# Gated linear attention by a cumulative log-decay over each chunk, in front of a two-expert router

## The chip, the cores and the metric

The kernel runs on one core of a Trainium2 chip. Its time is the device time of one execution in microseconds (us); the metric is the median of the runs.

## The reference

The first half is a gated linear recurrence for 4 batches, 8 heads, 768 tokens and 48 channels a head. The second half sends every token to its two best of 8 experts.

```
f = sigmoid(f_logit)                        # f_logit: normal, mean 2, spread 0.5
for t in range(S):
    state = f[t][:, None] * state + outer(k[t], v[t])     # 48 x 48 for each batch and head
    y[t]  = q[t] @ state
x = y, heads side by side                   # 3072 tokens x 384
noisy = x @ w_gate + softplus(x @ w_noise) * noise
top2 of noisy, weights = softmax over the two
out = sum over the two experts of weight * relu(x @ w1[e]) @ w2[e]     # 384 -> 1024 -> 384
```

All numbers are 32-bit floats.

## The kernel before, in words

The tokens are cut into 6 chunks of 128 per batch, so there are 24 pieces (chunk `c`, batch `b`), each with all 8 heads. Two heads share the 128 partitions (rows 0 to 47 and 64 to 111), so a piece has four pairs of heads, laid side by side as 4 x 128 columns.

**One piece** (`chunk`, L151 to L256). The sync queue SP loads `f`, `q`, `k`, `v`, the first three into one of three sets of padded tiles. TensorE (PE) transposes `f`, `q` and `k` (L166), four transposes each; ScalarE (ACT) takes the sigmoid (L170). The scores inside the chunk are built in seven levels, l = 0 to 6. Level l computes for each head the product of half the queries (64 columns) with the keys (L205), and VectorE (DVE) copies those that belong to the level into the score matrix `A` through a mask (L211; the last level by ACT, L213). Between levels the queries are multiplied by products of the decays on DVE (L215), and the keys and the decay products on GpSimd (POOL, L217, L219). A separate product gives the diagonal (L189, L191). A 32-bit matmul stands in the trace as two instructions, a transpose as one, so a level has 16 of them. Then `y` is made from `A` and `v` (L226) and from the carried state (L230, not for c = 0), and the state is carried on: the keys are transposed back (L240), multiplied with `v` (L247), and the old state is scaled and added (L254, L255; not in the last chunk).

**The order.** `by_turns` lets two streams of pieces alternate, two batches in each; it yields after the diagonal, after every level and after `y`. When the four pieces of a chunk are done, `pack` moves `y` by 10 DMAs into rows of 128 features (L265), and `route` (L270) transposes it to tokens, writes it out (`x_rows`), computes the router's logits (L285), the top two (a softplus out of Exp and Ln, then an Exp, L290 to L303), and scatters the tokens into expert lists by 8 indirect DMAs of the POOL queue (L343). The next chunk follows. Instructions of one engine run in the order in which the tile framework's scheduler has put them, near the program's order.

**The experts.** `plan` (L350) turns the counts into 55 tiles of 128 list entries. For each tile the token rows are gathered (L395), transposed (L407), sent through both layers (L417, L431), and added to the output rows (L426, L434, L436). Weights are fetched three tiles ahead (L401, L402). The output is cleared at the start by 24 DMAs that the POOL queue issues (L454).

PSUM is eight banks of 2 KB a partition: four single ones under the name `one`, two pairs under `two`.

Of the kernel before, what the change touches and what calls it, by code (L numbers as in the profile page):

```python
# [8 lines left out]
F32 = mybir.dt.float32  # L9
U8 = mybir.dt.uint8  # L10
U32 = mybir.dt.uint32
# [6 lines left out]

@with_exitstack
def kernel(  # L20
    ctx: ExitStack,
    tc: tile.TileContext,
    q: bass.AP,
    k: bass.AP,
    v: bass.AP,
    f_logit: bass.AP,
    moe_w_gate: bass.AP,
    moe_w_noise: bass.AP,
    moe_noise: bass.AP,
    moe_w1: bass.AP,  # L30
    moe_w2: bass.AP,
    out: bass.AP,
):

# [23 lines left out]
    C = 128  # L58
# [7 lines left out]
    TB = B * C  # L66
    NB = (2 * N - E) // 128 + E
    NR = 3
    FAR = 1 << 20
    assert (H * D, H * DP, 1 << NL, B * S) == (DM, 512, C, N) and TB == 512  # L70
# [4 lines left out]
    rt = ctx.enter_context(tc.tile_pool(name="rt", bufs=2))  # L75
    ffn = ctx.enter_context(tc.tile_pool(name="ffn", bufs=3))
# [29 lines left out]

    def counting(name, pattern, base=0, by_partition=0):
        t = const.tile([128] + [n for _, n in pattern], F32, tag=name, name=name)
        nc.gpsimd.iota(t, pattern=pattern, base=base, channel_multiplier=by_partition,
                       allow_small_or_imprecise_dtypes=True)  # L110
        return t

    iota = counting("iota", [[1, E]])
    list_of = counting("list_of", [[N, E]])
    token = counting("token", [[C, NCH], [S, B]], by_partition=1)
    start_of = counting("start_of", [[128, N // 128]])
    block = counting("block", [[1, NB]])

    ones = const.tile([128, 128], F32, tag="ones", name="ones")
    nc.gpsimd.memset(ones, 1.0)  # L120
    earlier = const.tile([128, 128], F32, tag="earlier", name="earlier")
    nc.gpsimd.affine_select(out=earlier, in_=ones, compare_op=ALU.is_ge, fill=0.0, base=-1,
                            pattern=[[1, 128]], channel_multiplier=-1)


    LR = E * N + 128
    x_rows = tc.dram_tile([N, DM], F32, name="x_rows")
    lists = tc.dram_tile([LR, 4], U32, name="lists")
    empty = const.tile([128, LR // 128, 4], U32, tag="empty", name="empty")
    for i, val in enumerate((0, FAR, 0, FAR)):  # L130
        nc.vector.memset(empty[:, :, i], val)
    nc.sync.dma_start(out=lists.rearrange("(p r) w -> p r w", p=128), in_=empty)

# [9 lines left out]

    xT = [None] * NCH
    before = const.tile([128, NCH * B + 1, E], F32, tag="before", name="before")
    nc.vector.memset(before[:, 0, :], 0.0)
    state = [None] * B
# [122 lines left out]
    def route(c):  # L270
        def t(shape, tag, dtype=F32):
            return rt.tile([128] + shape, dtype, tag=tag, name=f"{tag}_{c}")

        for b in range(B):
            xp = one_bank(f"xp_{c}_{b}")
            for i in range(KO):
                nc.tensor.transpose(xp[:, i * 128:(i + 1) * 128], xT[c][:, i, b * C:(b + 1) * C], ident)
            xs = t([DM], "xs")
            nc.scalar.copy(xs, xp[:, 0:DM])
            nc.sync.dma_start(out=x_rows[b * S + c * C:b * S + (c + 1) * C, :], in_=xs)  # L280

        lg = one_bank(f"lg_{c}")[:, 0:B * 2 * E].rearrange("t (b e) -> t b e", b=B)
# [11 lines left out]
        nc.vector.tensor_tensor(sp, sp, noise[:, c], ALU.mult)  # L294
        nc.vector.tensor_tensor(nz, sp, lg[:, :, 0:E], ALU.add)
        mx, ix, fx = t([B, 8], "mx"), t([B, 8], "ix", U32), t([B, 8], "fx")
        for b in range(B):
# [141 lines left out]

    def by_turns(*streams):  # L440
        streams = [iter(x) for x in streams]
        while streams:
            for x in list(streams):
                if next(x, streams) is streams:
                    streams.remove(x)

    def chunks(c, bs):
        for b in bs:
            yield from chunk(c, b)

# [59 lines left out]
```

## Time and profile before

| | |
|---|---|
| runs | 1420.2, 1413.39, 1419.17 us; median 1419.17 |
| profiled execution | 1423.89 us, its span 1422.2 us |
| mean granted clock of TensorE | 0.783 of full speed |
| PE busy | 1178.9 us (83%), 8391 instructions |
| ACT / DVE / POOL busy | 189.6 / 357.8 / 448.1 us |
| attention, to the last matmul of `y` | 0 to 692.8 us |
| from there to the first matmul of the experts | 692.8 to 740.1 us |
| experts | 740.1 to 1422.2 us |

The busy share alone says that TensorE is nearly full, but it is a mean over two very different stages: in the attention most of TensorE's instructions use a part of the array at half the clock, in the experts they use all of it at nearly the full clock.

### The profile page before, as it was taken

The numbers are of one execution on the slowest core, as the hardware profiler recorded it, in microseconds if no ns is written. First come the engines' busy times: TensorE is split into PE (matmuls) and PEld (weight loads), VectorE is DVE, ScalarE is ACT, GpSimd is POOL, SyncE is SP. The second block draws the span as 40 slices with busy tenths as digits, with TensorE's granted clock in tenths as the row PEclk, the third lists the DMA queues.
The fourth block names the chain that finished last, engine by engine and source line by source line (L and its number), as shares of the span: only waits on it lengthen the run. The fifth ranks groups of instructions, "written<-read, shape, count | busy, mean of one in ns | idle before, by whom it ended". The sixth has DMA issues, their size and how long they took to land. (4 is left out here: it accounts for less than half of the span.)

```text
span 1422.2 us, 21155 instructions
## 1 busy us (share of the span) xinstructions
PE 1178.9 (83%) x8391; PEld 953.1 (67%) x8391; DVE 357.8 (25%) x814; ACT 189.6 (13%) x322; POOL 448.1 (32%) x663
## 2 busy tenths in 40 slices
PE   3596797799599689789728889998989989999997
PEld 3585685666477568577526667776777767777775
DVE  2362552543345255245120000010100000011000
ACT  1013012111210301211100101010111101011110
POOL 9741430531323233062031222322222222222331
PEclk9976555555555555565559999999999999999999
DMA  9124022221211402210144635427163453637110
GB/s 194 54 46 86 5 45 56 35 45 35 56 23 24 90 1 45 56 18 6 36 162 148 211 124 192 142 90 245 45 215 128 143 196 118 234 109 256 51 40 7
DMA packets 163107, 135.64 MB, mean 95 GB/s; under 512 B 115909, under 2 KB 144249, under 8 KB 163008
## 3 DMA queue, kind: packets, MB, share of 16 engines
q1 hardware_dynamic: 149184, 104.34, 25.7%
q0 software_dynamic: 13824, 29.94, 6.9%
q8 instruction: 67, 1.10, 0.3%
q14 instruction: 32, 0.26, 0.1%
HBM read 213.75 MB, written 20.74 MB: 165 GB/s over the span
## 5 line engine op out<-in xcount | busy, mean ns | idle before, releaser
L417 PEld LDWEIGHTS hp<-xt,w 128*128 128x128 f32 x2640 | 317.6, 197 | 49.9 <-ACT hs L420 34.5
L417 PE MATMUL hp<-xt,w 128*128 128x128 f32 x2640 | 327.5, 282 | 23.9 <-ACT hs L420 23.3
L205 PE MATMUL sc<-qP,kQ 48*128 48x64 f32 (+1 forms) x2688 | 274.0, 392 | 82.4 <-DVE A L191 43.3
L205 PEld LDWEIGHTS sc<-qP,kQ 48*128 48x128 f32 (+1 forms) x2688 | 263.2, 301 | 93.0 <-DVE A L191 44.7
L431 PE MATMUL yp<-w,hs 128*128 128x384 f32 x880 | 294.6, 488 | 0.0
L431 PEld LDWEIGHTS yp<-w,hs 128*128 128x128 f32 x880 | 163.7, 191 | 102.9 <-issue 1.7
L211 DVE COPY_PREDICATED A<-masks,sc 128x512 f32<-128x512 uint8 x144 | 130.5, 906 | 115.2 <-PE sc L205 86.1
L420 ACT ACTIVATE hs<-hp 128x512 f32<-128x512 f32 x110 | 65.7, 597 | 631.3 <-PE hp L417 623.7
L436 POOL DMA_INDIRECT out_dram<-ys,slots x55 | 55.6, 1011 | 295.8 <-DVE ys L434 295.4
L434 DVE SCALAR_TENSOR_TENSOR ys<-yp,slots,had 128x384 f32<-128x384 f32 x55 | 34.0, 618 | 446.1 <-PE yp L431 314.7
L217 POOL TENSOR_TENSOR kQ<-kQ,T 128x256 f32<-128x256 f32 x140 | 94.8, 677 | 137.4 <-PE sc L205 137.2
L343 POOL DMA_INDIRECT lists<-entry,sloti x48 | 46.9, 977 | 208.6 <-DVE sloti L340 195.8
L426 POOL DMA_INDIRECT had<-out_dram,slots x55 | 57.0, 1036 | 174.6 <-issue 138.3
L409 DVE COPY xt<-xgp 128x384 f32<-128x384 f32 x55 | 30.7, 558 | 183.5 <-PE xgp L407 183.5
L407 PE MATMUL xgp<-ident,xg 128*128 128x128 f32 x165 | 29.7, 291 | 49.5 <-DMA xg<-x_rows,slots 49.5
L215 DVE TENSOR_TENSOR qP<-qP,T 128x256 f32<-128x256 f32 x144 | 62.2, 432 | 11.3 <-PE sc L205 10.4
L395 POOL DMA_INDIRECT xg<-x_rows,slots x55 | 53.4, 971 | 30.7 <-issue 19.4
L226 PE MATMUL y<-A,v 128*48 128x128 f32 x384 | 60.1, 428 | 0.0
L213 ACT COPY A<-sc 64x512 f32<-64x512 f32 x24 | 13.9, 578 | 336.8 <-DVE qP L215 326.1
L407 PEld LDWEIGHTS xgp<-ident,xg 128*128 128x128 f32 x165 | 20.3, 148 | 51.7 <-issue 32.2
L230 PE MATMUL y<-qP,st 48*48 48x128 f32 x320 | 53.3, 432 | 0.0
L226 PEld LDWEIGHTS y<-A,v 128*48 128x48 f32 x384 | 25.1, 175 | 26.5 <-issue 25.0
(119 smaller groups left out, 767.6 us busy)
## 6 DMA issues: line engine op xcount, KB each, us to landing
w<-in_moe_w_dram SPq DMA_DIRECT2D x110, 1536.0 KB
f<-in_f_logit_dram SPq DMA_DIRECT2D x24, 192.0 KB
q<-in_q_dram SPq DMA_DIRECT2D x24, 192.0 KB
k<-in_k_dram SPq DMA_DIRECT2D x24, 192.0 KB
v<-in_v_dram SPq DMA_DIRECT2D x24, 192.0 KB
out_dram<-zero POOLq DMA_DIRECT2D x24, 192.0 KB, 2.2
x_rows<-xs SPq DMA_DIRECT2D x24, 192.0 KB
xT<-yT SPq DMA_DIRECT2D x36, 96.0 KB
```

Source lines behind the costliest of these rows:

```text
L205: nc.tensor.matmul(sc[0:nj, par, hp * HC:(hp + 1) * HC].rearrange("j (a m) -> j a m", m=m), lhsT=kQ[rows(par), hp * C:hp * C + nj], rhs=qv ...
L211: nc.vector.copy_predicated(Av, masks[:, l].rearrange("j (r x m) -> j r x m", r=2, m=m), scv)
L215: nc.vector.tensor_tensor(qv, qv, Tv[:, :, 0:1].broadcast_to((128, x, m)), ALU.mult)
L217: nc.gpsimd.tensor_tensor(kv, kv, Tv[:, :, 1:2].broadcast_to((128, x, m)), ALU.mult)
L226: nc.tensor.matmul(y[rows(par), par, cols(hp)], lhsT=vt[:, 2 * hp + par, :], rhs=A[:, par, cols(hp)], start=True, stop=(c == 0))
L230: nc.tensor.matmul(y[rows(par), par, cols(hp)], lhsT=state[b][rows(par), hp, :], rhs=qP[rows(par), cols(hp)], start=False, stop=True)
L395: nc.gpsimd.indirect_dma_start(out=xg, out_offset=None, in_=x_rows, in_offset=bass.IndirectOffsetOnAxis(ap=slots[:, 0:1], axis=0))
L417: nc.tensor.matmul(hp[:, fo // 4, fo % 4, :], lhsT=w1[t % NR][:, i, fo * 128:(fo + 1) * 128], rhs=xt[:, i, :], start=(i == 0), stop=(i == ...
L420: nc.scalar.activation(hs[:, fo - 3:fo + 1, :], hp[:, fo // 4], AF.Relu)
L426: nc.gpsimd.indirect_dma_start(out=had, out_offset=None, in_=out, in_offset=bass.IndirectOffsetOnAxis(ap=slots[:, 1:2], axis=0), bounds_ch ...
L431: nc.tensor.matmul(yp[:, 0:DM], lhsT=hs[:, fo, :], rhs=w2[t % NR][:, fo, :], start=(fo == 0), stop=(fo == FO - 1))
L436: nc.gpsimd.indirect_dma_start(out=out, out_offset=bass.IndirectOffsetOnAxis(ap=slots[:, 3:4], axis=0), in_=ys, in_offset=None, bounds_che ...
```

## The change

The seven levels are replaced by one product. With L the running sum of -ln(f) inside the chunk, the decay from key j to query i is exp(-(L_i - L_j)). So the queries are multiplied by P = exp(-L), the keys by Q = exp(L), one matmul per head gives all 128 x 128 scores, and one multiplication with a causal mask makes `A`. L comes from Exp, Ln (ACT) and a running sum along the columns (`tensor_tensor_scan` on DVE, which starts again at each pair of heads and is capped at 60). The state is carried as P at the chunk's end times (old state + keys times `v`).

The pieces run as five stages with a lag each, in one loop over 24 steps and a few more, and `pack` is gone: the logits are computed straight from `y` with the router's weights laid out by pairs of heads, for each piece as it comes, in one PSUM bank that is held from the first batch's piece to `route`. The loads are four sets deep. At the very end a register is loaded and a branch decides on a redo of everything by the general method: it is taken if any channel's sum over a chunk exceeded 39. `plan` and all of the experts' part keep their text.

```diff
+    def load(n):
+        c, b = n // B, n % B
+        for nm, src in (("f", f_logit), ("q", q), ("k", k), ("v", v)):
+            nc.sync.dma_start(out=pads[nm][n % NLD][:, :, 0:D],
+                              in_=src[b, :, c * C:(c + 1) * C, :].rearrange("h t d -> t h d"))
...
+    def forget(n):
+        raw = pads["f"][n % NLD].rearrange("t h d -> t (h d)")
+        nc.gpsimd.tensor_scalar(raw, raw, XMIN, None, ALU.max)
+        f = wk.tile([128, HP * C], F32, tag="f", name=f"f_{n}")
+        nc.scalar.activation(f, transposed("f", n), AF.Exp, scale=-1.0)
+        nc.scalar.activation(f, f, AF.Ln, bias=1.0)
+        L = wk.tile([128, HP * C], F32, tag="L", name=f"L_{n}")
+        top = cap[n % 2]
+        nc.gpsimd.tensor_copy(top[:, :, 0], f.rearrange("d (a t) -> d a t", t=C)[:, :, 0])
+        nc.vector.tensor_tensor_scan(L, data0=f, data1=top.rearrange("d a t -> d (a t)"), initial=0.0,
+                                     op0=ALU.add, op1=ALU.min)
+        P[n] = wk.tile([128, HP * C], F32, tag="P", name=f"P_{n}", bufs=4)
+        nc.scalar.activation(P[n], L, AF.Exp, scale=-1.0)
+        Q[n] = wk.tile([128, HP * C], F32, tag="Q", name=f"Q_{n}")
+        nc.scalar.activation(Q[n], L, AF.Exp)
+        nc.gpsimd.tensor_copy(far[:, n, :], L.rearrange("d (a t) -> d a t", t=C)[:, :, C - 1])
+    def scaled(n):
+        qP[n] = wk.tile([128, HP * C], F32, tag="qP", name=f"qP_{n}", bufs=3)
+        nc.vector.tensor_tensor(qP[n], transposed("q", n), P[n], ALU.mult)
+        kQ[n] = wk.tile([128, HP * C], F32, tag="kQ", name=f"kQ_{n}")
+        nc.vector.tensor_tensor(kQ[n], transposed("k", n), Q[n], ALU.mult)
+    def scores(n):
+        sc = two_banks(f"sc_{n}")
+        for hp in range(HP):
+            for par in range(2):
+                nc.tensor.matmul(sc[:, par, cols(hp)], lhsT=kQ[n][rows(par), cols(hp)],
+                                 rhs=qP[n][rows(par), cols(hp)], start=True, stop=True)
+        A[n] = wk.tile([C, 2, HP * C], F32, tag="A", name=f"A_{n}")
+        nc.vector.tensor_tensor(A[n].rearrange("j r (a i) -> j (r a) i", i=C), sc.rearrange("j r (a i) -> j (r a) i", i=C),
+                                causal.unsqueeze(1).broadcast_to((C, H, C)), ALU.mult)
+        if n // B < NCH - 1:
+            kp = one_bank(f"kp_{n}")
+            for hp in range(HP):
+                nc.tensor.transpose(kp[:, cols(hp)], kQ[n][:, cols(hp)], ident)
+            kn[n] = wk.tile([C, H, DP], F32, tag="kn", name=f"kn_{n}")
+            nc.scalar.copy(kn[n].rearrange("t h d -> t (h d)"), kp)
+    def output(n):
+        c, b = n // B, n % B
+        vt = pads["v"][n % NLD]
+        y = one_bank(f"y_{n}")
+        for hp in range(HP):
+            for par in range(2):
+                nc.tensor.matmul(y[rows(par), cols(hp)], lhsT=vt[:, 2 * hp + par, :], rhs=A[n][:, par, cols(hp)],
+                                 start=True, stop=(c == 0))
+            if c:
+                for par in range(2):
+                    nc.tensor.matmul(y[rows(par), cols(hp)], lhsT=state[b][rows(par), hp, :],
+                                     rhs=qP[n][rows(par), cols(hp)], start=False, stop=True)
+        yT[n] = wk.tile([128, HP * C], F32, tag="yT", name=f"yT_{n}")
+        nc.scalar.copy(yT[n], y)
+        if c == NCH - 1:
+            return
+        ds = one_bank(f"ds_{n}")
+        for hp in range(HP):
+            for par in range(2):
+                nc.tensor.matmul(ds[rows(par), hp * DP:(hp + 1) * DP], lhsT=kn[n][:, 2 * hp + par, :],
+                                 rhs=vt[:, 2 * hp + par, :], start=True, stop=True)
+        dsv = ds[:, 0:HP * DP].rearrange("d (a e) -> d a e", e=DP)
+        end = P[n].rearrange("d (a t) -> d a t", t=C)[:, :, C - 1:C].broadcast_to((128, HP, DP))
+        new = wk.tile([128, HP, DP], F32, tag=f"st{b}", name=f"st_{n}")
+        if c == 0:
+            nc.vector.tensor_tensor(new, dsv, end, ALU.mult)
+        else:
+            mid = wk.tile([128, HP, DP], F32, tag="mid", name=f"mid_{n}")
+            nc.vector.tensor_tensor(mid, dsv, state[b], ALU.add)
+            nc.gpsimd.tensor_tensor(new, mid, end, ALU.mult)
+        state[b] = new
+    def features(n):
+        c, b = n // B, n % B
+        xp = one_bank(f"xp_{n}")
+        for hp in range(HP):
+            nc.tensor.transpose(xp[:, cols(hp)], yT[n][:, cols(hp)], ident)
+        xs = wk.tile([128, H, D], F32, tag="xs", name=f"xs_{n}")
+        nc.scalar.copy(xs, xp.rearrange("t (h d) -> t h d", d=DP)[:, :, 0:D])
+        nc.sync.dma_start(out=x_rows[b * S + c * C:b * S + (c + 1) * C, :], in_=xs.rearrange("t h d -> t (h d)"))
+        if b == 0:
+            lg[c] = one_bank(f"lg_{c}")[:, 0:B * 2 * E].rearrange("t (b e) -> t b e", b=B)
+        for hp in range(HP):
+            nc.tensor.matmul(lg[c][:, b, :], lhsT=yT[n][:, cols(hp)], rhs=w_rt[:, hp, :],
+                             start=(hp == 0), stop=(hp == HP - 1))
...
+    def beyond():
+        ok = rt.tile([128, NCH * B * HP], F32, tag="ok", name="ok", bufs=1)
+        nc.gpsimd.tensor_scalar(ok, far.rearrange("d n a -> d (n a)"), LMAX, None, ALU.is_le)
+        low = rt.tile([128, 1], F32, tag="low", name="low", bufs=1)
+        nc.vector.tensor_reduce(low, ok, axis=AX.X, op=ALU.min)
+        count = one_bank("count")
+        nc.tensor.matmul(count[0:1, 0:1], lhsT=low, rhs=ones[:, 0:1], start=True, stop=True)
+        nc.vector.tensor_scalar(bad, count[0:1, 0:1], 127.5, None, ALU.is_lt)
...
-    for c in range(NCH):
-        yT[c] = wk.tile([128, HP, B, C], F32, tag="yT", name=f"yT{c}", bufs=1)
-        by_turns(chunks(c, range(0, B, 2)), chunks(c, range(1, B, 2)))
-        xT[c] = wk.tile([128, KO, TB], F32, tag="xT", name=f"xT{c}")
-        pack(c)
-        route(c)
+    NS = NCH * B
+    for n in range(NLD):
+        load(n)
+    for i in range(-2, NS + 2):
+        for stage, lag in ((forget, -2), (scaled, -1), (scores, 0), (output, 1), (features, 2)):
+            n = i - lag
+            if 0 <= n < NS:
+                stage(n)
+                if stage is output and n + NLD < NS:
+                    load(n + NLD)
+                if stage is features and n % B == B - 1:
+                    route(n // B)
+    beyond()
+    att.close()
+    ffn = ctx.enter_context(tc.tile_pool(name="ffn", bufs=3))
...
+    ctx.close()
+    with tc.If(nc.values_load(bad, min_val=0, max_val=1, skip_runtime_bounds_check_because="it is 0 or 1") > 0):
+        with ExitStack() as inner:
+            general(inner, tc, q, k, v, f_logit, moe_w_gate, moe_w_noise, moe_noise, moe_w1, moe_w2, out)
```

`general` holds the attention as it was before and runs all 8 experts over all tokens. `beyond` compares the 96 columns of `far` with 39 and counts the partitions that are within, by one small matmul.

## Rows read from the trace of the kernel before

**Rows 1.** Stretches: us; busy us (instructions) of each engine; TensorE's clock; DMA share; GB/s.
```profile
0.00:692.80 692.80, 543.05 (x4664) 450.24 (x4664) 283.73 (x648) 117.13 (x201) 251.67 (x438) 0.61 0.23 47
692.80:740.10 47.30, 10.99 (x45) 9.28 (x45) 9.90 (x57) 6.83 (x12) 9.91 (x10) 0.50 0.29 94
740.10:1422.20 682.10, 624.87 (x3682) 493.61 (x3682) 64.12 (x110) 65.67 (x110) 186.53 (x215) 0.98 0.43 144
```

**Rows 2.** The costliest group of the attention: line, engine, operation, shapes, count; busy us, mean ns; idle before.
```profile
L205 PE MATMUL sc<-qP,kQ 48*128 48x64 f32 (+1 forms) x2688 | 274.0, 392 | 82.4 <-DVE A L191 43.3
```

**Rows 3.** Shorter stretches of the attention, and the first 40 us.
```profile
0.00:40.00 40.00, 13.65 (x88) 11.35 (x88) 10.04 (x28) 4.82 (x7) 39.26 (x56) 1.00 0.88 192
196.00:250.00 54.00, 44.59 (x352) 36.19 (x353) 20.46 (x63) 9.79 (x17) 9.00 (x13) 0.50 0.14 38
302.00:305.20 3.20, 3.20 (x23) 3.11 (x21) 0.51 (x2) 1.18 (x2) 0.85 (x2) 0.50 0.43 84
305.30:308.70 3.40, 3.21 (x46) 2.80 (x45) 2.11 (x4) 1.39 (x3) 1.22 (x6) 1.00 0.89 154
```

**Rows 4.** TensorE in order of time, 183 to 195 us: start, length, line, count.
```profile
183.57 1.10 PE L247 MATMUL ds<-v,kn 128*64 128x48 f32 x16 [0.68 <-ACT kn L242]
184.59 1.12 PE L166 MATMUL fp<-ident,f 128*128 128x128 f32 x4
186.36 1.06 PE L166 MATMUL kp<-ident,k 128*128 128x128 f32 x4
...
189.79 0.67 PE L247 MATMUL ds<-v,kn 128*64 128x48 f32 x16
190.39 0.66 PE L166 MATMUL fp<-ident,f 128*128 128x128 f32 x4
...
191.32 0.60 PE L166 MATMUL kp<-ident,k 128*128 128x128 f32 x4
192.76 1.16 PE L189 MATMUL diag<-qT,kQ 48*128 48x128 f32 x16 [0.84 <-ACT kQ L177]
```

**Rows 5.** TensorE at other places: `y`, state, diagonal.
```profile
105.99 3.65 PE L226 MATMUL y<-A,v 128*48 128x128 f32 x32
217.90 0.67 PE L226 MATMUL y<-A,v 128*48 128x128 f32 x4
218.50 0.67 PE L230 MATMUL y<-qP,st 48*48 48x128 f32 x4
654.31 2.08 PE L189 MATMUL diag<-qT,kQ 48*128 48x128 f32 x16
```

**Rows 6.** Groups that price the new work of ACT, DVE and POOL.
```profile
L170 ACT ACTIVATE f<-fp 128x512 f32<-128x512 f32 x24 | 14.5, 604 | 45.4 <-PE fp L166 38.5 <-POOL kQ L217 6.8
L191 DVE TENSOR_TENSOR A<-diag,ident 128x1024 f32<-128x1024 f32 x24 | 29.2, 1219 | 10.1 <-PE diag L189 10.1
L175 DVE TENSOR_TENSOR qP<-qp,f 128x512 f32<-128x512 f32 x24 | 16.6, 692 | 40.1 <-ACT qT L173 32.4 <-PE y L230 7.6
L361 DVE TENSOR_TENSOR_SCAN upto<-ones,nblk 128x8 f32<-128x8 f32 x1 | 0.2, 163 | 0.0
L217 POOL TENSOR_TENSOR kQ<-kQ,T 128x256 f32<-128x256 f32 x140 | 94.8, 677 | 137.4 <-PE sc L205 137.2
L454 POOL DMA_DIRECT2D out_dram<-zero x24 | 13.4, 560 | 0.0
```

**Rows 7.** ACT in order of time, inside `route` of the first chunk.
```profile
125.12 1.28 ACT L291 ACT_TABLE_LOAD   x1
126.42 0.23 ACT L291 ACTIVATE sp<-sp 128x32 f32<-128x32 f32 x1
...
127.03 1.28 ACT L292 ACT_TABLE_LOAD   x1
```

**Rows 8.** The end of the attention, in order of time.
```profile
702.55 5.30 PE L285 MATMUL lg<-w_rt,xT 128*128 128x16 f32 x24
...
729.63 0.36 SPq L393 DMA_DIRECT2D slots<-lists  x1
```

More of the change, by code (lines that the diff above doesn't have):

```diff
@@ L16, with general @@
 PSUM = bass.MemoryType.PSUM
[L19 to L33, printed above, removed]
+def general(ctx, tc, q, k, v, f_logit, moe_w_gate, moe_w_noise, moe_noise, moe_w1, moe_w2, out):
     nc = tc.nc
@@ L105 @@
         nc.gpsimd.tensor_copy(masks[:, l], mf)
[L107 to L132, printed above, removed]
+    iota = const.tile([128, E], F32, tag="iota", name="iota")
+    nc.gpsimd.iota(iota, pattern=[[1, E]], base=0, channel_multiplier=0, allow_small_or_imprecise_dtypes=True)
     w_rt = const.tile([128, KO, 2 * E], F32, tag="w_rt", name="w_rt")
@@ L295, in route @@
         nc.vector.tensor_tensor(nz, sp, lg[:, :, 0:E], ALU.add)
+        mx, ix, fx = t([B, 8], "mx"), t([B, 8], "ix", U32), t([B, 8], "fx")
+        for b in range(B):
+            nc.vector.max(out=mx[:, b, :], in_=nz[:, b, :])
+            nc.vector.max_index(out=ix[:, b, :], in_max=mx[:, b, :], in_values=nz[:, b, :])
+        nc.vector.tensor_copy(fx, ix)
+        ex, sm = t([B, 2], "ex"), t([B, 1], "sm")
+        nc.vector.tensor_tensor(ex, mx[:, :, 0:2], mx[:, :, 0:1].broadcast_to((128, B, 2)), ALU.subtract)
@@ new lines, in route @@
+        nc.scalar.activation(ex, ex, AF.Exp)
+        nc.vector.tensor_tensor(sm, ex[:, :, 0:1], ex[:, :, 1:2], ALU.add)
+        nc.vector.tensor_scalar_add(sm, sm, 1e-9)
+        nc.vector.reciprocal(sm, sm)
+        nc.vector.tensor_tensor(ex, ex, sm.broadcast_to((128, B, 2)), ALU.mult)
+        hot = [t([B, E], "hot0"), t([B, E], "hot1")]
+        for r in range(2):
+            nc.vector.tensor_tensor(hot[r], iota.unsqueeze(1).broadcast_to((128, B, E)),
+                                    fx[:, :, r:r + 1].broadcast_to((128, B, E)), ALU.is_equal)
+            nc.vector.tensor_tensor(hot[r], hot[r], ex[:, :, r:r + 1].broadcast_to((128, B, E)), ALU.mult)
@@ new lines, in route, with load_expert @@
+        nc.vector.tensor_tensor(gate[c], hot[0], hot[1], ALU.add)
+    def load_expert(e):
+        w1, w2 = [], []
+        for s in range(2):
+            w = wts.tile([128, KO, HALF * 128], F32, tag="w1", name=f"w1_{e}_{s}")
+            nc.gpsimd.dma_start(out=w, in_=moe_w1[e, :, s * HALF * 128:(s + 1) * HALF * 128].rearrange(
+                "(k p) f -> p k f", p=128))
+            w1.append(w)
+        for s in range(2):
+            w = wts.tile([128, HALF, DM], F32, tag="w2", name=f"w2_{e}_{s}")
+            nc.gpsimd.dma_start(out=w, in_=moe_w2[e, s * HALF * 128:(s + 1) * HALF * 128, :].rearrange(
+                "(f p) d -> p f d", p=128))
+            w2.append(w)
+        return w1, w2
@@ new lines, in expert @@
+    def expert(e, c, w1, w2):
+        h = []
+        for fo in range(FO):
+            hp = one_bank(f"hp_{e}_{c}_{fo}")
+            w, o = w1[fo // HALF], (fo % HALF) * 128
+            for i in range(KO):
+                nc.tensor.matmul(hp, lhsT=w[:, i, o:o + 128], rhs=xT[c][:, i, :], start=(i == 0), stop=(i == KO - 1))
+            hs = hid.tile([128, TB], F32, tag="h", name=f"h_{e}_{c}_{fo}")
+            nc.scalar.activation(hs, hp, AF.Relu)
+            h.append(hs)
+            yield
+        for b in range(B):
+            yp = one_bank(f"yp_{e}_{c}_{b}")
+            for fo in range(FO):
+                nc.tensor.matmul(yp[:, 0:DM], lhsT=h[fo][:, b * C:(b + 1) * C], rhs=w2[fo // HALF][:, fo % HALF, :],
+                                 start=(fo == 0), stop=(fo == FO - 1))
+            a, g = acc[c][:, b, :], gate[c][:, b, e:e + 1]
+            if e == 0:
+                nc.vector.tensor_scalar(a, yp[:, 0:DM], g, None, ALU.mult)
+            else:
+                nc.vector.scalar_tensor_tensor(a, in0=yp[:, 0:DM], scalar=g, in1=a, op0=ALU.mult, op1=ALU.add)
+            if e == E - 1:
+                nc.sync.dma_start(out=out[b * S + c * C:b * S + (c + 1) * C, :], in_=a)
+            yield
@@ new lines, in by_turns, with chunks @@
+    def by_turns(*streams):
+        streams = [iter(x) for x in streams]
+        while streams:
+            for x in list(streams):
+                if next(x, streams) is streams:
+                    streams.remove(x)
+    def chunks(c, bs):
+        for b in bs:
+            yield from chunk(c, b)
+    load_router()
+    for c in range(NCH):
+        yT[c] = wk.tile([128, HP, B, C], F32, tag="yT", name=f"yT{c}", bufs=1)
+        by_turns(chunks(c, range(0, B, 2)), chunks(c, range(1, B, 2)), expert(0, c - 1, *w) if c else ())
+        if c == 0:
+            w = load_expert(0)
+        pack(c)
+        route(c)
```

153 lines of the change are left out of this document (130 added, 23 removed).

## The prediction

> **What bounds the kernel now.** I read the stretches first. The attention takes 692.8 us, 28.9 us for each of its 24 pieces, the passage to the experts 47.3 us, the experts 682.1 us [rows 1]. With 1.7 us outside the span that is the profiled execution's own 1423.9 us. In the attention PE is busy 543 of 692.8 us at a mean clock of 0.61, in the experts 625 of 682 us at 0.98, and no other engine comes near half. So both stages are bound by PE, and the change touches the first alone. The costliest group there is the level products of L205, 274.0 us [rows 2]; DVE comes behind it, waiting for PE.
>
> The clock matters as much as the count. Stretches full of L205 have a granted clock of 0.50; after a run of transposes it is 1.00 for a short while [rows 3]. What that is worth stands side by side: twelve transposes take 2.83 us at 184.59 (to the end of the row at 186.36) and 1.53 us at 190.39 (to the end of the row at 191.32); `ds` takes 1.10 and 0.67 us [rows 4], the diagonal's sixteen 2.08 us [rows 5] and 1.16 us [rows 4]. The two levels are 1.2 and 2.4 GHz.
>
> **PE's work for a piece afterwards.** All 112 instructions of L205 and the 16 of the diagonal go. What is left or new, at the low clock and at the high one:
> - twelve transposes of `f`, `q`, `k`: 2.83 and 1.53 us.
> - scores, 16 instructions of the diagonal's form but 64 rows high: 2.08 and 1.16 us.
> - `y` with the state: four groups of `y` and four of the state, 0.60 us apart [rows 5], so 4.78 us; in the first chunk, without the state, half of 3.65 us. Mean 4.29 us. No row has the pair at the high clock: between 2.15 (half) and 4.29, I take 2.4, by the ratio of the diagonal.
> - keys turned back (four transposes) and `ds`, in 20 of 24 pieces: 1.1 + 1.2 and 0.65 + 0.75 us, mean 1.9 and 1.2. `ds` has 64 columns for 48, hence a little more than its row.
> - four transposes of `y` (1.1 and 0.65) and 8 of the logit instructions. 24 of those took 5.30 us [rows 8], so 1.77 us; at the high clock between 0.9 and 1.77, I take 1.0.
> - a share of `route`'s rank products, 0.3 and 0.2.
>
> Together 14.3 us at the low clock, 8.1 at the high one.
>
> **The other engines, a piece.** ACT: an Exp from PSUM 0.604 us [rows 6]; Ln, P and Q have the same 512 columns, 0.6 each; three copies out of PSUM, together 1.6: 4.0 us. Exp and Ln follow each other in each piece, and in `route` the trace has a table load before the Exp of L291 and another before the Ln of L292, 1.28 us each [rows 7]; so two loads a piece, 2.57 us. `route` adds at most the passage's 6.83 us of ACT for every four pieces [rows 1], which includes five copies already counted; I take 1.1. Sum 7.7 us. In the trace the load begins at 125.12 and the Exp at 126.42 [rows 7], 1.30 us in all, so I charge the load and nothing beside it. The Trainium skill, page "ScalarE: Activation LUTs", section "What ACT_TABLE_LOAD costs", adds 1380 ns of drain to each switch; here the trace does not agree with it.
>
> DVE: two products out of PSUM at 0.692, the causal product 1.219, the state's sum about 0.4 and the scan. The scan is in the trace only at 8 columns, 0.163 us [rows 6]. At the least it costs as a plain pass over 512 columns, 0.69; at the most, if all of the 0.163 grew with the columns, 64 times that, 10.4 us. An 8-column row is mostly fixed cost, so I stay near the plain pass and take 1.2. With `route` (at most 9.9 us for four pieces [rows 1]) DVE has 5 to 6.5 us. At the upper end of the scan it would have 15 and be the bound.
>
> POOL: the maximum on `f` and the state's product, by L217's 0.677 about 0.7 each (up to 1.4 if the maximum costs by the column), two tiny copies, and 8 scatters for four pieces: some 4 us. Loads (four inputs of 3072 x 384 numbers), row writes, the clearing and the empty lists are by the shapes 28.7 MB; at the first 40 us' 192 GB/s [rows 3] that is 150 us, below the 200 and more that the other engines need. `pack`'s 60 DMAs leave SP's queue, and loads no longer stand behind them.
>
> **The wait that the change adds.** P and Q wait for the scan, which waits for Ln and for a small copy on POOL, where a scatter of 1 us may be ahead. Queued behind P on ACT are the copies that free PSUM banks. Of the four `one` banks one is held by the logits nearly always, so PE can run at most three results ahead. The stages are a step apart, so this costs no whole chain but some tenths in a step; I add 0.3 us.
>
> **The step.** L205, in which the clock fell, is gone; the transposes, after which it rose, stay and are now 20 of some 90 PE instructions. At the low clock PE has no idle time (14.3 against 7.7 on ACT), so it will rise; at the high clock PE and ACT are nearly level (8.1 and 7.7), so PE has gaps, and the stretch of logits and waits may let it fall. I take a third of the work at the low clock: (14.3 + 2 x 8.1) / 3 = 10.2, with the waits 10.5 us a piece.
>
> **The sum**, against 1423.9:
> - Lead-in to the first scores 18 us. The first transposes ran at about 4 us, and one piece's chain (transposes, Exp, load, Ln, scan, load, P, Q, two products) adds about 9; the rest is loads that share the DMAs with the clearing, which fill them to 0.88 in the first 40 us [rows 3]. If the first maximum stands behind all 24 clearing issues (13.4 us [rows 6]) and the router's loads on POOL, it is 30; without any hindrance 13.
> - 24 x 10.5 = 252 us.
> - Passage 36 us. Before, `y` ended at 692.8 and the logits at 707.85 [rows 8], 15.1 us for copies, `pack`, transposes and four batches' logits. After it is one copy 0.6, four transposes 1.1 and one batch's logits 1.8, so 11.6 us go from 47.3. The rest, `route`, scatters, plan, first fetch, is unchanged and as exposed as before.
> - Experts 682 us: same text, same bound.
> - The end: register load on each engine, a branch over the redo. No row shows a branch. Nothing as the lower bound; the nearest exposed rows are single round trips, such as the wait before `slots` at 729.63 [rows 8], some 3 us, and six of them in a row would be 20. I take 8. The Trainium skill, page "Runtime: NRT & Kernel Launch", section "Instruction fetch mechanics", says a taken branch to a page not at hand waits for that page to be fetched; no row here shows it.
> - Outside the span 1.7.
>
> 18 + 252 + 36 + 682 + 8 + 1.7 = 998 us. The profiled execution lay 4.7 us above the median of the runs, so I predict 993.
>
> **Rivals.**
> 1. The clock stays low in the attention (the mean there was 0.61 [rows 1]). Then 14.3 us a piece, +91 us: 1084. For it: scores, `y` and state use 64 of 128 rows or columns. Against: the full transposes come every step.
> 2. The clock stays high throughout: PE and ACT near 8.2, with waits 8.5, -48 us: 945. For it: 8.1 of 8.5 us busy is as dense as the experts. Against: the logits' slow weight loads and the bank waits.
> 3. Stages run into one another, through the held bank or a slow scan, at 12 to 25 us a piece: 1030 to 1345. Even without any overlap at the low clock a piece adds up to about 26 us (14.3 of PE, 6.6 of ACT, 5 of DVE), less than 28.9; this alone cannot make it slower.
> 4. Slower: the redo is taken. Place: the branch at the end; it decides from any channel whose sum over 128 tokens exceeds 39. Price: the attention as before, 693 us, and 8 experts x 24 blocks = 192 tiles where 55 took 682 us, 2380 us at the same rate: about 4000 us in all. Against: -ln f at a logit of 2 is 0.127, with the spread about 0.14 in the mean, 18 in a chunk, and 39 is far outside its spread.
> 5. A table switch between two long passes stops ACT for longer than in `route`, say for a second 1.28 us: 2.75 switches a piece make ACT 7.7 + 3.5 = 11.2 us, +17 us: 1010. The 1.30 us from load to Exp [rows 7] speaks against it. The page on ScalarE named above would have it so, and with its figure the sum would be about 1017.
>
> **Chances.** Forecast 0.52, rival 1 0.16, rival 2 0.18, rival 3 0.09, rival 4 0.02, rival 5 0.02, the rest (change has no effect) 0.01. The forecast's own range, 9.3 to 12 us a piece with the lead-in's and the end's bounds, is 955 to 1040; for 8 in 10 I go out to rival 2's lower end, 938, and rival 1, 1086. A measurement here tells about 0.5% from no change; only rival 4 is slower by that: faster 0.97, same 0.01, slower 0.02.
>
> **What would show it.** Attention ending near 270 us with pieces 10 us apart; ACT busy 6.5 to 8 us in each; two table loads of 1.28 us a piece; the scan between 0.7 and 1.7 us; the clock between 0.6 and 0.9 there; first expert matmul 36 us after the last `y`; experts 682 us; the last write some microseconds before the end. It is wrong in mechanism if DVE or the DMAs set the step, if the experts' stage changes, or if the end costs more than 20 us.

## The result and the profile after

The changed kernel takes 1024.46 us in the median of four runs (1021.94 to 1035.0), the kernel before 1417.6 on the same chip: a ratio of 0.7243, 95% interval 0.7189 to 0.7297. The forecast was 993 with a range from 938 to 1086. The profiled execution took 1024.36 us, its span 1022.6, at a mean granted clock of 0.911. In e1 and e7 below one run, and in e5 and e11 two, lay over 1.5% above the fastest of their kernel; the ratios leave these slow runs out, the medians do not.

The stretches of the changed kernel, as in [rows 1]: from and to, length, then for PE, PEld, DVE, ACT and POOL the busy us with the number of instructions, TensorE's granted clock, DMA share, GB/s.

```profile
0.00:28.80 28.80, 0.00 (x0) 0.00 (x0) 3.85 (x27) 1.28 (x1) 23.25 (x51) 1.00 1.10 281
28.80:40.20 11.40, 6.66 (x28) 5.56 (x28) 4.36 (x5) 7.68 (x11) 8.86 (x9) 0.92 1.24 131
40.20:303.60 263.40, 222.00 (x2034) 169.32 (x2034) 112.97 (x322) 157.63 (x227) 83.82 (x119) 0.79 0.37 73
303.60:337.00 33.40, 6.66 (x32) 6.39 (x32) 8.69 (x56) 4.97 (x9) 10.97 (x13) 0.50 0.23 76
337.00:1013.50 676.50, 623.63 (x3685) 492.11 (x3685) 64.66 (x110) 65.67 (x110) 185.35 (x215) 0.98 0.44 147
```

The first scores start at 40.2 us; TensorE has done nothing for 28.8 us, while POOL was busy. The 24 pieces then take 263.4 us, 10.97 each, against 28.9 before. The 10.97 is a mean over two sorts of step. From one piece's scores to the next's, the steps run 8.1, 6.7, 16.9, 16.2 us, and much the same in every chunk once the first `route` has come (the six steps ahead of it have 7.0 on average). Here is one such round, by the same view, cut at the starts of the scores:

```profile
179.06:196.00 16.94, 11.98 (x111) 9.57 (x110) 8.18 (x47) 9.93 (x15) 4.52 (x7) 0.80 0.29 60
196.00:212.16 16.16, 12.70 (x93) 9.51 (x92) 5.22 (x6) 8.06 (x11) 8.58 (x11) 0.70 0.46 86
212.16:220.30 8.14, 8.14 (x93) 6.26 (x92) 3.72 (x6) 5.63 (x10) 2.48 (x4) 0.98 0.57 119
220.30:227.00 6.70, 6.70 (x83) 4.92 (x82) 3.81 (x5) 5.65 (x8) 1.79 (x3) 1.00 0.52 100
```

A plain step is TensorE from end to end, at the full clock. The two long ones follow `route`: in the first TensorE is busy 12 of 17 us, in the second POOL 8.6 of 16, and in both the clock falls. In the first, TensorE stands at the rank product (the view of waits: engine, line, waited for, total, times, longest; and the place in order of time):

```profile
PE rk L604 <- DVE late L610: 23.6, 5, 4.7
```
```profile
184.94 0.60 PE L604 MATMUL rk<-both,earlier 128*128 128x32 f32 x2 [4.71 <-DVE late L610]
```

In the second, the scatters stand on POOL ahead of the small copy `cap` of the next piece, and DVE's and ACT's queues behind that copy. Four of the eight start in the first long step and four in the second (start, length, engine, line; in brackets the idle time before it and its releaser):

```profile
191.40 1.07 POOL L627 DMA_INDIRECT lists<-entry,sloti  x1 [0.54 <-DVE kQ L502]
...
200.37 0.95 POOL L627 DMA_INDIRECT lists<-entry,sloti  x1 [0.31 <-issue]
201.91 0.19 POOL L489 COPY cap<-f 128x4 f32<-128x4 f32 x1
202.13 1.63 DVE L490 TENSOR_TENSOR_SCAN L<-f,cap 128x512 f32<-128x512 f32 x1
203.69 1.19 DVE L511 TENSOR_TENSOR A<-sc,causal 128x1024 f32<-128x1024 f32 x1
203.80 0.63 ACT L493 ACTIVATE P<-L 128x512 f32<-128x512 f32 x1 [2.86 <-DVE L L490]
204.85 0.56 ACT L518 COPY kn<-kp 128x512 f32<-128x512 f32 x1
```

The copy's input was written at 199.64 (ACT's logarithm), the copy ran at 201.91; the scan waits for it, DVE's `A` and ACT's P behind the scan, and ACT's PSUM copies behind P. Of the 8.2 us that this step is longer than a plain one, TensorE is idle for 3.5 (16.16 less 12.70); the other 4.7 are the slower work at a clock of 0.70.

### The profile page after: what moved, and what is told of

Same layout as the page of the kernel before. It is cut to its first block, busy times and chain, and to the rows that moved or that the text cites. A ratio compares the mean times of both kernels' runs of the same rounds, so it can differ in the third digit from the quotient of the medians.

```text
span 1022.6 us, 14847 instructions
## 1 busy us (share of the span) xinstructions
PE 859.0 (84%) x5777; PEld 673.4 (66%) x5777; DVE 194.5 (19%) x519; ACT 237.2 (23%) x357; POOL 312.3 (31%) x406
## 5 line engine op out<-in xcount | busy, mean ns | idle before, releaser
L526 PE MATMUL y<-A,v 128*64 128x128 f32 x384 | 47.5, 333 | 5.1 <-issue 4.8
L482 POOL TENSOR_SCALAR f<-f 128x512 f32<-128x512 f32 x24 | 36.6, 1527 | 31.4 <-DMA f<-in_f_logit_dram 31.3
L477 PE MATMUL fp<-ident,f 128*128 128x128 f32 x96 | 20.7, 355 | 29.2 <-POOL f L482 29.2
L530 PE MATMUL y<-qP,st 64*64 64x128 f32 x320 | 42.0, 343 | 1.7 <-issue 1.7
L490 DVE TENSOR_TENSOR_SCAN L<-f,cap 128x512 f32<-128x512 f32 x24 | 30.0, 1255 | 48.4 <-POOL cap L489 47.6
L526 PEld LDWEIGHTS y<-A,v 128*64 128x64 f32 x384 | 21.9, 153 | 23.0 <-issue 22.1
L477 PEld LDWEIGHTS fp<-ident,f 128*128 128x128 f32 x96 | 16.4, 205 | 29.6 <-POOL f L482 29.6
L530 PEld LDWEIGHTS y<-qP,st 64*64 64x64 f32 x320 | 18.6, 154 | 21.0 <-issue 21.0
L508 PE MATMUL sc<-qP,kQ 64*128 64x128 f32 x384 | 31.9, 312 | 0.0
```

Source lines behind the costliest of these rows:

```text
L477: nc.tensor.transpose(p[:, cols(hp)], flat[:, cols(hp)], ident)
L482: nc.gpsimd.tensor_scalar(raw, raw, XMIN, None, ALU.max)
L526: nc.tensor.matmul(y[rows(par), cols(hp)], lhsT=vt[:, 2 * hp + par, :], rhs=A[n][:, par, cols(hp)], start=True, stop=(c == 0))
L530: nc.tensor.matmul(y[rows(par), cols(hp)], lhsT=state[b][rows(par), hp, :], rhs=qP[n][rows(par), cols(hp)], start=False, stop=True)
```

## The experiments

The times of all runs (us), with the step structure read from the traces. "Scores" is from the first piece's scores to the last's, 23 steps.

| run | median | ratio to before, interval | first scores | scores |
|---|---|---|---|---|
| changed kernel | 1024.5 | 0.7243 [0.7189, 0.7297] | 40.2 | 248.7 |
| e1_clear_late | 1015.7 | 0.7161 [0.7117, 0.7205] | 20.7 | 251.0 |
| e2_rank_late | 995.2 | 0.6985 [0.6928, 0.7042] | 40.7 | 211.4 |
| e3_no_scatter | 982.2 | 0.6936 [0.6887, 0.6985] | 40.3 | 211.3 |
| e4_no_branch | 1028.0 | 0.7227 [0.7176, 0.7278] | 40.7 | 247.7 |
| e5_pool_busy | 1021.9 | 0.7157 [0.7089, 0.7224] | 40.2 | 244.5 |
| e6_filler | 1027.8 | 0.7263 [0.7212, 0.7313] | 40.4 | 237.8 |
| e7_combined | 942.6 | 0.6604 [0.6547, 0.6661] | 20.7 | 190.6 |
| e8_no_tables | 938.9 | 0.6610 [0.6554, 0.6666] | 20.7 | 190.9 |
| e9_combined | 954.8 | 0.6727 [0.6700, 0.6755] | 21.0 | 202.6 |
| e10_dve_cap | 1006.5 | 0.7085 [0.7059, 0.7111] | 17.6 | 247.7 |
| e11_all | 957.0 | runs 943.4 to 963.3 | 18.5 | 205.0 |
| e12_pool_free | 988.1 | 0.6966 [0.6912, 0.7021] | 17.6 | 226.4 |

Some runs do not do the whole work: e3 and e5 leave out all scatters of the first five chunks, e7 and e8 the last two of the eight in each of these chunks, and e8 also the logarithm.

The experts' stage, whose text is the same in all, varied from 670 to 686 us, from its first matmul to its last, between these profiled runs; so a mechanism is read from its own stretch, the total only where the gain is larger.

### The lead-in

In the changed kernel POOL issues the clearing and the router's loads ahead of the first maximum:

```profile
5.26 4.52 POOL L736 DMA_DIRECT2D out_dram<-zero  x8 [1.65 <-DVE prev L614]
...
20.64 0.54 POOL L736 DMA_DIRECT2D out_dram<-zero  x1 [0.30 <-DMA out_dram<-zero]
...
23.88 3.31 POOL L450 DMA_DIRECT2D noise<-in_moe_noise_dram  x4
27.27 5.87 POOL L482 TENSOR_SCALAR f<-f 128x512 f32<-128x512 f32 x4
```

The later clearings wait for earlier ones to land, and the maximum starts at 27.27.

```diff
-    for i in range(0, N, 128):
-        nc.gpsimd.dma_start(out=out[i:i + 128, :], in_=zero)
-    load_router()
 ...
+        if i == -2:
+            load_router()
+        if 0 <= i < NS:
+            nc.gpsimd.dma_start(out=out[i * 128:(i + 1) * 128, :], in_=zero)
```

> The 24 clearing writes of the output are issued one to a step inside the loop, and the router's weights after the first step, instead of all ahead of the first load. Theory: the lead-in of 40.2 us is set by POOL's queue, where the first maximum stands behind 28 us of these issues; then the first scores come 11 to 15 us after the first loads have landed, near 20 to 25 us, the steps stay as they are, and the time falls by 15 to 20 us from 1024.5, to 1004 to 1010. Rival: the first loads themselves, all 16 of them at once, or the chain behind the maximum set it; then the first scores come later than 32 us and the time falls by less than 8 us. A second rival: 24 issues inside the steps cost what they save (24 x 0.6 us = 14 us on POOL), the lead-in shortens and the steps lengthen, and the time is within 5 us of 1024.5.

The first maximum and the first scores, in order of time:

```profile
4.12 1.54 POOL L482 TENSOR_SCALAR f<-f 128x512 f32<-128x512 f32 x1 [0.50 <-DMA f<-in_f_logit_dram]
```
```profile
20.66 1.26 PE L508 MATMUL sc<-qP,kQ 64*128 64x128 f32 x16
```

The first maximum ran at 4.12 instead of 27.27, the first scores started 19.6 us earlier, and the steps stayed as they were (251.0 against 248.7). The profiled execution took 1005.2, the median of the four runs was 1015.7. Both rivals fall for the lead-in; the total bears out a gain, though its interval still overlaps that of the changed kernel.

### The wait for the ranks

`route` becomes a generator that stops ahead of the rank product; its second half follows one step later.

```diff
+        yield
         rk = one_bank(f"rk_{c}")[:, 0:B * E].rearrange(...)
 ...
-                    route(n // B)
+                    ranks = route(n // B)
+                    next(ranks)
+        if i % B == (B + 2) % B and i > B + 1 and i < NS:
+            next(ranks, None)
```

> The second half of the routing (rank products, list slots, scatters) comes one step later than the first half (softplus, top two, softmax), so TensorE does not reach the rank product before its operands are there. Theory: TensorE's wait of 4.7 to 4.9 us at the rank product, in five of the 24 steps, is lost time; it goes, the first of the two slow steps after each routing falls from 17 to 11 or 12 us, and the time falls by 20 to 25 us from 1024.5, to 1000 to 1005. Rival: the wait is a symptom, the slow pair of steps is set by the eight scatters and by the low clock; then the sum of the two steps after the routing (33 us) falls by under 2 us each time and the time by under 8 us.

The step with the first half of `route` and the next, which now has ranks and scatters:

```profile
166.80:176.50 9.70, 8.73 (x99) 6.66 (x98) 8.55 (x48) 6.64 (x12) 2.50 (x4) 1.00 0.54 105
176.50:190.90 14.40, 9.73 (x93) 6.79 (x92) 4.75 (x7) 6.79 (x10) 10.25 (x12) 0.85 0.35 54
```

17 became 9.7 us at clock 1.00, the step with all eight scatters took 14.4, and all scores together fell by 37.3 us, more than the theory's 20 to 25; the median fell by 29. The wait is lost time, not a symptom.

How much of the long step is clock? A second experiment keeps the order and lets TensorE work while it would wait:

```diff
+        for i in range(28):
+            nc.tensor.transpose(bank[:, 128 + 128 * (i % 3):256 + 128 * (i % 3)], ident, ident)
         nc.tensor.matmul(rk, lhsT=earlier, ...)
```

> Adds 28 transposes of a constant ahead of the rank product (4.6 us at the high clock, 7.7 at the low one), so TensorE works while it would wait for the router; their result is not used. Theory: the first slow step after each routing (17 us against 8) holds 4.9 us of waiting and 4 us that TensorE loses at the low clock behind it; with TensorE kept busy the clock stays high and the step falls to 12 to 14 us, 15 to 25 us over five routings, though 28 instructions were added. Rival: the clock falls anyway or the chain through ACT and POOL sets the step; then it stays at 17 us or rises, and the time is within 8 us of 1024.5 or above it.

The filler moved ahead of the scores, so the two steps are to be read together (13.30 + 8.20 us):

```profile
215.30:228.60 13.30, 11.68 (x127) 9.53 (x126) 7.95 (x46) 10.03 (x16) 2.45 (x4) 1.00 0.40 77
228.60:236.80 8.20, 8.14 (x93) 6.03 (x92) 3.94 (x7) 5.43 (x8) 3.77 (x6) 1.00 0.32 56
```

They last 21.5 us where the changed kernel has 6.6 + 16.9 = 23.5, with the clock at 1.00 throughout; in two other rounds the pair took 22.1 and 22.0 against 23.8 and 23.6, and in the round that is left it ran into the scatters' step and can't be told apart. So of the 7.5 us that this pair is longer than two plain steps of 8, the low clock is 2 us, half of what I expected, and most of the rest is the 4.7 us of waiting. All scores together fell by 10.9 us, less than the theory's 15 to 25, and the total did not move by more than the runs differ.

### The scatters

Leave them out for five chunks:

```diff
-        for b in range(B):
+        for b in range(B if c == NCH - 1 else 0):
```

> Leaves out the eight scatters of the first five chunks (40 of 48), so most tokens are missing in the lists; the experts' stage still runs its 55 tiles but reads placeholder entries, so only the attention, to the last product of y, is compared. Theory: while the eight scatters are under way, TensorE's results are released 1 to 6 us after the matmuls' recorded ends; without them this lag is gone, the second slow step after each routing falls from 16.4 to 7 to 9 us and part of the first with it, and the attention of 263.4 us falls by 35 to 60 us. Rival: the lag belongs to the stop before (TensorE's wait at the rank product and the clock that falls behind it) and the scatters only lie beside it; then the second slow step stays above 13 us and the attention falls by less than 15 us.

The two steps after `route`:

```profile
161.60:178.60 17.00, 12.29 (x109) 9.90 (x108) 8.31 (x48) 10.74 (x17) 2.98 (x5) 0.80 0.36 80
178.60:186.60 8.00, 8.00 (x93) 6.08 (x92) 4.07 (x6) 6.40 (x10) 2.45 (x4) 1.00 0.69 126
```

The second fell from 16.2 to 8.00, a plain step, TensorE busy all of it, and all scores together fell by 37.4 us, within the theory's 35 to 60; the first kept its 17, so the part "of the first with it" was wrong. Whether it is the transfer or POOL's time, the next run tells: POOL does as much without a transfer.

```diff
+        if c < NCH - 1:
+            nc.gpsimd.tensor_copy(scratch[:, 0:1], slot[:, 0, 0:1])
+            for _ in range(2 * B):
+                nc.gpsimd.tensor_scalar(scratch, scratch, 0.0, None, ALU.max)
```

> Leaves out the scatters of the first five chunks, as the run without scatters did, and puts in their place on POOL, behind the same slots, nine passes without any transfer, eight of them 128 x 420 (some 1.25 us each, 10 us in all); only the attention is compared. Theory: the step with the scatters is 16.4 instead of 8.0 us because POOL, busy for 9 to 10 us, keeps the small copy (cap) of the next piece waiting, and the scan, P, Q and the scores behind it; then POOL's passes do the same without a transfer, and that step is 15 to 17 us again. Rival: the scatters' transfers delay TensorE's results, which were released 1 to 6 us late only while scatters ran; then without transfers the step is 8 to 10 us, as in the run without scatters.

The step, and in it the copy, the scan (two lines further down in this kernel, L491 and L492) and the next stop of TensorE, behind ACT's copy `kn`:

```profile
193.70:209.20 15.50, 10.49 (x95) 8.37 (x94) 4.36 (x6) 7.20 (x10) 9.28 (x11) 0.74 0.36 65
```
```profile
200.82 0.19 POOL L491 COPY cap<-f 128x4 f32<-128x4 f32 x1
201.04 1.23 DVE L492 TENSOR_TENSOR_SCAN L<-f,cap 128x512 f32<-128x512 f32 x1 [6.35 <-POOL cap L491]
203.98 1.11 PE L558 MATMUL xp<-ident,yT 128*128 128x128 f32 x4 [5.01 <-ACT kn L520]
```

15.5 us without any transfer: POOL's occupation alone makes the long step (15.7, 15.6 and 14.4 in the other rounds). Its four runs, 1009.6 to 1029.7 us, all lie above the four without scatters, 979.7 to 992.3. Then the reverse, the scatters left in a row and the pieces' work taken off POOL, first the copy and the maximum:

```diff
-        nc.gpsimd.tensor_scalar(raw, raw, XMIN, None, ALU.max)
+        nc.vector.tensor_scalar(raw, raw, XMIN, None, ALU.max)
 ...
-        nc.gpsimd.tensor_copy(top[:, :, 0], ...)
+        nc.vector.tensor_copy(top[:, :, 0], ...)
```

> The changed kernel with one thing moved: the small copy (cap) and the maximum on f go from POOL to VectorE, so the chain from f to the scores no longer passes POOL; the eight scatters stay in a row, and the clearing and the ranks stay where they are. Theory: the scatters cost 8.4 us a chunk only because the next piece's copy stands behind them on POOL; then the step with the scatters falls from 16.4 to 8 to 10 us as without scatters, and the lead-in falls too (no maximum behind the clearing), to about 21 us; together 45 to 60 us less than 1024.5. Rival: TensorE's results come late while scatters run, whatever POOL's queue holds; then the step stays at 13 us or more and only the lead-in's 19 us go.

Neither: the step fell from 16.4 to 12.7, 13.2 and 12.6 in three rounds, at the rival's 13 rather than the theory's 10, and to 8.0 in the fourth. The theory's 45 to 60 us did not come either: the median fell by 18. The first scores started 22.6 us earlier, but the second step took 18.6 us where the changed kernel has 6.6, so all scores together fell by only 1.0. In that step DVE, which now has the maximum in its queue, waited for a load of `f`:

```profile
27.88 0.43 DVE L482 TENSOR_SCALAR f<-f 128x512 f32<-128x512 f32 x1 [3.98 <-DMA f<-in_f_logit_dram]
```

What else lengthened it is not tested. In a step with scatters of the same run, ACT waited for this:

```profile
187.43 0.63 ACT L493 ACTIVATE P<-L 128x512 f32<-128x512 f32 x1 [1.49 <-POOL st L549]
```

P has four buffers, and the oldest was still to be read by POOL's `st`, behind the scatters. So the next run moves `st` and `far` as well:

```diff
-            nc.gpsimd.tensor_tensor(new, mid, end, ALU.mult)
+            nc.vector.tensor_tensor(new, mid, end, ALU.mult)
 ...
-        nc.gpsimd.tensor_copy(far[:, n, :], ...)
+        nc.vector.tensor_copy(far[:, n, :], ...)
```

> As e10_dve_cap, with the two POOL operations that were left in a piece moved to VectorE as well (the state's product st and the copy far), so that between the scatters POOL has nothing that a piece waits for; clearing, ranks and the eight scatters in a row stay. Theory: what was left of the scatters' cost in e10_dve_cap (12.7 us for 8) is still POOL's queue: P waits for a buffer that st and far, behind the scatters, have not read yet, and ScalarE's copies stand behind P; then the step with the scatters falls to 8 to 9.5 us, five times 3 to 4 us less than e10_dve_cap, near 990. Rival: the rest is the low clock behind the wait for the ranks, or the scatters' transfers themselves; then the step stays at 11.5 to 13 us and the time within 5 us of 1006.5.

```profile
170.90:178.90 8.00, 8.00 (x95) 6.10 (x94) 4.13 (x7) 6.40 (x10) 4.36 (x4) 1.00 0.84 124
```

8.00 us, in all four places where the next scores end such a step. Of the eight scatters of this round five start in the step before and three in this one:

```profile
164.78 1.62 POOL L627 DMA_INDIRECT lists<-entry,sloti  x1 [29.09 <-DVE sloti L624]
...
175.20 0.97 POOL L627 DMA_INDIRECT lists<-entry,sloti  x1 [0.30 <-issue]
```

The step before takes 17.2 us, as it does without scatters (17.0 in e3), so the scatters themselves cost nothing that these two steps show; their place in POOL's queue did. The median of 988.1 is near the theory's 990 in part by luck: of the 21.3 us that all scores fell against e10, these four steps have 14.6, the second step (11.1 instead of 18.6) has 7.5, and one step behind the scatters took 13.3, in which DVE waited 4.5 us for a load of `f`.

### The end

```diff
-    with tc.If(nc.values_load(bad, ...) > 0):
-        with ExitStack() as inner:
-            general(inner, tc, ...)
```

> Leaves out the branch at the end and the general method behind it, which is never entered with these inputs; the flag is still computed. Theory: register loads and branch cost what the end is longer than before, 3.9 us; the time falls by 3 to 5 us from 1024.5, and the last 11 us of the span become 7. Rival as I forecast it: 8 us. Rival: the branch costs nothing and the end is longer because of the writes' own landing; then the time stays within 1.5 us.

The last product of the experts, in the changed kernel (span 1022.6) and without the branch (span 1029.4):

```profile
1011.64 0.62 DVE L718 SCALAR_TENSOR_TENSOR ys<-yp,slots,had 128x384 f32<-128x384 f32 x1 [10.91 <-PE yp L715]
```
```profile
1022.31 0.62 DVE L718 SCALAR_TENSOR_TENSOR ys<-yp,slots,had 128x384 f32<-128x384 f32 x1 [10.91 <-PE yp L715]
```

11.0 us follow it with the branch, 7.1 without, as before the change: 3.9 us. In the total it cannot be seen: the medians differ by 3.5 us the other way, and the intervals of the ratios overlap.

### Together, and ACT's table loads

e7 and e9 have the late clearing, the late ranks, and the scatters issued in pairs, between which the small POOL operations come; e7, and e8 with it, leave out the last pair of the first five chunks:

```diff
+            yield                       # after each batch's two scatters
 ...
+        if i > begun:
+            next(ranks, None)
```

> Late clearing and late ranks together, and the eight scatters of a chunk in pairs with the pieces' small POOL operations between them instead of in a row. Theory: the three gains stand in different places and add up: 19 us of lead-in, 39 us of attention by the late ranks, and the scatter step from 14.4 to 9 to 11 us, five times 4 to 5 us, so 940 to 955 us. Rival: with the waits gone ACT's table loads and the DMAs become the bound, steps stay near 10 us and the gain stops at 960 to 975. Second rival: the scatters cost the same wherever they stand; then 965.

> As the combined kernel, but the logarithm over 128 x 512 is replaced by a copy of the same size, so the decay sums are those of exp(-x) and ScalarE needs no table load for a piece (the two for each routing stay). Theory as in my prediction: PE and ACT are nearly level, PE sets a plain step of 7 to 8 us, and ACT's 2.57 us of loads lie in the chain but two pieces deep; then the attention falls by less than 15 us against the combined kernel. Rival: the loads are in the chain from f to the scores that sets the steps; then 24 x 2.57 us, up to 60 us, go, and steps fall to 5 to 6 us.

> The combined kernel with all 48 scatters: in e7_combined and e8_no_tables as they ran, the last two of the eight scatters of the first five chunks were left out, so a quarter of those chunks' tokens did not reach the lists. Theory: the attention steps are as there, 8 us plain and 9 to 11 us with scatters, the two more scatters cost under 1 us a chunk, so 942 to 952 us. Rival: eight scatters hold POOL longer than the gaps in one step and the step with them rises above 12 us; then 955 to 965.

Three steps of e7, and the same three of e8, where the logarithm is a copy:

```profile
129.90:158.30 28.40, 26.59 (x283) 19.86 (x282) 17.29 (x58) 19.75 (x32) 14.53 (x19) 0.94 0.52 95
```
```profile
130.50:158.50 28.00, 26.63 (x281) 20.17 (x280) 17.12 (x58) 14.55 (x28) 15.91 (x20) 0.94 0.50 96
```

ACT lost 5.2 us of work in three steps, TensorE's did not change and the steps lost 0.4; all scores took 190.9 against 190.6 us. After the first six steps the sums are equal, 144.2 us each, so there the loads are off the path. In the first six, which have less work, it is not shown: the first three of e8 took 17.7 us against 23.6, but its fourth 14.1, in which POOL waited 4.4 us for a load of `f`.

e7's 942.6 lies within the theory's 940 to 955, but without the ten scatters. With all of them (e9) three of the four chunks whose steps the scores' starts show have one step of 11.8 to 13.2 us again, and the median is 954.8, beyond the theory's 952 and at the edge of the rival's 955: 0.6727 of before against 0.7243 for the change. As the rival said, POOL is held: in one such step the copy, whose input was written at 167.45, stood behind the last scatter, the maximum and `st`.

```profile
167.45 0.95 POOL L628 DMA_INDIRECT lists<-entry,sloti  x1 [0.30 <-issue]
170.69 1.22 DVE L490 TENSOR_TENSOR_SCAN L<-f,cap 128x512 f32<-128x512 f32 x1 [3.98 <-POOL cap L489]
```

> The combined kernel of e9_combined with the copy and the maximum on VectorE as well. Theory: TensorE at the high clock sets 8 us a step everywhere and nothing waits for POOL; 1 to 2 us go from the five steps with scatters, so 5 to 10 us less than e9_combined. Rival: VectorE, some 0.9 us fuller in each piece, delays the products behind it in its queue and eats that: within 4 us of e9_combined.

957.0 and 954.8 with overlapping runs: no difference that these runs can tell, so the rival's time came, but its reason was not tested; `st` and `far`, which e12 moved off POOL, still stood there.

## Why the prediction was right, and which terms were not

The sum goes by its own terms, forecast and measured: lead-in 18 and 40.2; pieces 252 and 263.4; passage 36 and 35.4 (303.6 to the first experts' matmul at 339.04); experts with the writes' landing 682 and 679.7; branch 8 and 3.9; outside 1.7. The differences, +22.2 +11.4 -0.6 -2.3 -4.1, are the 26.6 us between the sum (997.7 before rounding) and the profiled 1024.4. The attention, forecast to end near 270 us, ended at 303.6. The prediction's own range, 955 to 1040, is narrower than its bounds taken together, which give 951 to 1053; nothing hung on it.

**Lead-in: mis-sized, outside its own bounds of 13 to 30.** The sentence "If the first maximum stands behind all 24 clearing issues (13.4 us [rows 6]) and the router's loads on POOL, it is 30" named what happened, and the order stands in the program's text; I took the better case. It was 40 since the issues lasted longer than in [rows 6]: from 5.26 the clearing fills 16 us, part of it waiting for its own transfers, the router's loads 5.7, the maximum 1.5, and then the chain to the scores 11.4 instead of 9. With the cause removed it was 20.7 and 17.6.

**TensorE's work: right.** 8.1 us at the high clock was forecast for a piece; a plain step is 8.00 us of it. `y` and the state at the high clock, taken at 2.4 between 2.15 and 4.29, are eight groups 0.37 us apart, 2.95.

**The step: right in the mean by two errors.** I spread the low clock and 0.3 us of waits evenly over the pieces. In fact TensorE's work is 222.0 / 24 = 9.25 us a piece (10.2 forecast), and the waits are (263.4 - 222.0) / 24 = 1.7. A plain step runs at the full clock as rival 2 had it, and 7.5 us more for the ranks and 8.2 for the scatters in each chunk bring the mean back; that 10.97 lies near 10.5 is luck. The waits step failed: I counted "a scatter of 1 us may be ahead" where eight stood in a row, and of the rank product, which stands in TensorE's queue ahead of the next piece's transposes, I counted the work and not the wait. The kernel before has that wait too, in the passage for one:

```profile
714.31 0.61 PE L320 MATMUL rk<-both,earlier 128*128 128x32 f32 x2 [6.45 <-DVE late L326]
```

**ACT: right.** 6.6 us a piece, 7.7 in the sum with 6.5 to 8 as the sign, with two table loads of 1.28 us in each, and the scan at 1.2 (line, engine, operation; count; busy us, mean ns; idle before and its releaser):

```profile
L485 ACT ACT_TABLE_LOAD x22 | 28.2, 1283 | 0.4
L493 ACT ACT_TABLE_LOAD x22 | 28.2, 1283 | 0.4
L490 DVE TENSOR_TENSOR_SCAN L<-f,cap 128x512 f32<-128x512 f32 x22 | 27.3, 1242 | 17.8 <-POOL cap L489 17.1 <-issue 0.7
L482 POOL TENSOR_SCALAR f<-f 128x512 f32<-128x512 f32 x18 | 26.8, 1488 | 30.3 <-DMA f<-in_f_logit_dram 30.3
```

Rival 5 falls: from a load's start to its activation are 1.30 us (172.29 to 173.59) also between the long passes. The Trainium skill, page "ScalarE: Activation LUTs", section "What ACT_TABLE_LOAD costs", adds 1380 ns of drain to a switch; no row here shows it, and the 1.30 us leave no room for it. The maximum on POOL, 1.49 us, was taken at 0.7 and lies just above its bound of 1.4.

**Passage and experts: right**; the branch, taken at 8, is 3.9. "PE and ACT are nearly level" was too strong: ACT, busy 6.4 of the 8.0 us of a plain step, does not set it (e8).

## What to carry to other kernels

A mean over equal steps hides which of them stop: cut the trace at one instruction's starts and compare the windows. When work is moved into a pipelined loop, look for each engine at what stands in its queue ahead of the next piece's first instruction; a burst on an idle engine (here eight scatters on POOL, at a third busy) cost most of its length, 8.2 of 10 us, since a 0.2 us copy that starts the next chain was queued behind it. Prefetch and clearing issued "for free" ahead of a loop are not free on a queue that the loop's first instruction uses; off that queue, as in e10, the first scores came 22.6 us earlier, but a step behind them grew by 12 us.

## What the runs showed that I had not expected

While the scatters ran in the changed kernel, TensorE's results were taken later than the recorded ends of its matmuls allow:

```profile
194.64 0.66 PE L477 MATMUL qp<-ident,q 128*128 128x128 f32 x4
199.20 0.37 SPq L470 DMA_DIRECT2D q<-in_q_dram  x1
199.28 0.69 DVE L500 TENSOR_TENSOR qP<-qp,P 128x512 f32<-128x512 f32 x1 [4.69 <-PE kp L516]
```

The transposes of `q` end at 195.30 by the record, yet both that wait for them, DVE's product and the load that may then overwrite `q`, start at 199.2 to 199.3. The same is seen in each of four rounds, by 3.3 to 4.8 us, in the changed kernel, e1, e4 and e6. In e2, e10 and e12, which have the same eight scatters in a row, no such delay is seen, and e5 has the long step without a scatter and without the delay. So the delay is not needed for the long step; how much it adds in the changed kernel was not measured, and its cause is open. The granted clock reads 1.00 in that stretch.
